# Block 0's queries come by GpSimd's queue: a chunk-selecting attention with a SwiGLU layer behind it

## The chip, the core and the metric

The kernel runs on one core of one Trainium2 chip. A core has five engines with an instruction queue each: TensorE (PE, matrix products), VectorE (DVE), ScalarE (ACT), GpSimd (POOL) and SyncE (SP, which only issues transfers here). Transfers between HBM and on-chip memory are started by SP, ACT or POOL and are carried by 16 DMA engines that all three share. The metric is the device time of one execution in microseconds (us); lower is better.

## What is computed

For 4 batches, 8 heads, 768 positions and 64 features per head, attention looks only at the six best chunks of 32 keys for each query, where a chunk is ranked by an upper bound from the least and the greatest of its keys, feature by feature. Its output, put together over the heads, goes through an RMS norm and a SwiGLU layer with 512 inputs and 1536 hidden features.

```
k_min, k_max = min and max of k over each chunk of 32 positions
ub    = sum_d max(q * k_min, q * k_max)            # one bound per query and chunk, causal
top   = the 6 chunks with the largest ub
attn  = softmax(q k^T / 8, causal, only keys of the chunks in top)
x     = (attn v), heads side by side               # 3072 tokens x 512
xn    = x / sqrt(mean(x^2) + 1e-6) * rms_g
out   = (silu(xn w_gate) * (xn w_val)) w_out       # 512 -> 1536 -> 512
```

## The kernel before, in words

The work is cut into 12 blocks of 256 tokens, `ORDER` in the code: block 0 is batch 0's first 256 positions, block 1 batch 1's, and so on. A block is named in operations by batch and third, so `(0, 0)` is block 0, `(1, 0)` block 1, `(2, 0)` block 2, `(0, 1)` block 4; a third figure is the group of four heads, of which there are two.

For each block the steps are: load k, q and v (`load_qk`, line 431; `load_v`, line 456). VectorE turns k and q so that features lie on partitions (`turn k`, `turn q`, line 636); ScalarE or GpSimd makes 16-bit copies of them (`half`, lines 643 and 644). VectorE takes each chunk's least and greatest key (`ext0`, `ext1`, line 651), GpSimd or VectorE writes them into small matrices (`dk`, line 657; `bd0`, `bd1`, line 676), and TensorE makes the bounds with them (`upper`, line 540), for which q's positive part is needed too (`relu`, lines 731 and 733). VectorE ranks (`ubn`, `bar`, `top`, `mk`, `mt`, lines 565 to 591). TensorE makes scores (line 760, with the mask at 771), ScalarE the exponentials (`exp`, line 810), GpSimd clears what lies above the diagonal (`tri`, line 780), TensorE multiplies with the values (`values`, line 836), VectorE normalises (`rden`, `norm`, lines 851 and 855). Then come the RMS norm (`square`, `rms`, `scale`, `turn`, `xsT`, lines 872 to 929) and the SwiGLU layer (`ffn`: `wg`, `wv` at line 960, `tanh`, `tg`, `vcopy`, `hh`, and `project` at line 1007).

For the first two blocks the norm and the layer run on half blocks, so that `xsT(0, (0,))` is block 0's first 128 tokens, ready for the first real matrices of the layer. Before that, and in gaps, TensorE is kept at work with multiplications that nobody reads (line 1074); they need the identity matrix `ident`, which GpSimd writes.

The order of the work is not decided on the chip. `Plan` collects all operations, each with a number, and the list `STEPS` says in which order they are written to their engines' queues: an entry is eight times the operation's number plus the engine, and a negative entry is a run of fill multiplications. Each engine works through its own queue in order and waits, by semaphores, for what an operation reads. `SLOTS` names the buffer that each tile takes. Both lists come from a search over the operations' assumed durations, made ahead of time.

Loads of k and q of the first three blocks are four transfers each, of 32 partitions, 128 KB (`PACKED`). All weights and values come by GpSimd's queue, converted to 16 bits on the way: `wg0` is the first third of the gate weights, `v000` and `v001` the two halves of block 0's values. `HELD = {2: ("wg", 1), 3: ("wo", 0)}` adds two waits: block 2's first load may not be issued before `wg1` has landed, and block 3's not before `wo0`. There are two buffers for raw k and three for raw q.

In the order before, SP issues two loads of block 0's k and two of its q, then block 1's; ACT issues the other two of each. GpSimd's queue begins with small clears, `ident`, `wv0`, `v000`, `wg1`, `v001`, `v100`, `wg0`.

Of the kernel before, what the change touches and what calls it, by code (L numbers as in the profile page):

```python
# [33 lines left out]
class Plan:  # L34
# [213 lines left out]
def kernel(  # L248
# [41 lines left out]
    def at(key):  # L290
        return store[plan.pool_of[key]][plan.slot[key]]
# [814 lines left out]
```

## Time and profile before

| | |
|---|---|
| Median of 3 runs | 294.74 us (293.15 to 296.25) |
| The profiled execution | 293.79 us |
| Its span in the profile | 292.1 us |
| TensorE busy | 279.0 us of the span |
| VectorE, ScalarE, GpSimd busy | 215.7, 207.1, 167.8 us |

The profile is one execution. Its span runs from the first instruction to the last; 1.69 us of the execution's time lie around it. Engine names are those above; PEld is TensorE's loading of weights, and a q behind an engine's name means its queue, where transfers are issued. A row of the timeline has start, length, engine, line, operation, output<-input, shapes and count, and in brackets the idle time before it with what ended that. Busy matrix products include the fill.

### The profile page before, as it was taken

What the parts mean: (1) busy time and instruction counts of PE and PEld (TensorE: products, weight loads), DVE (VectorE), ACT (ScalarE), POOL (GpSimd) and SP (SyncE); (2) the same over time, 40 slices, a digit from 0 to 9 for tenths busy, and PEclk for the clock granted to TensorE, in tenths of its full rate; (3) what the DMA queues carried; (4) which work ended last, traced back from release to release, by engine and by line L of the source; (5) the groups of instructions that cost most, each with busy time, mean ns of one, the idle gap of its engine ahead of it and who ended that gap; (6) DMA issues with size and microseconds to landing.
All of it is one profiled execution on the core that took longest, in us unless ns stands there. A gap on an engine that the chain in (4) does not pass through costs nothing.

```text
span 292.1 us, 11448 instructions
## 1 busy us (share of the span) xinstructions
PE 279.0 (96%) x4718; PEld 214.8 (74%) x4746; DVE 215.7 (74%) x626; ACT 207.1 (71%) x355; POOL 167.8 (57%) x268
## 2 busy tenths in 40 slices
PE   7979999999999899999999999999999999999994
PEld 7637887668877757888676786688678967688663
DVE  3778887889898799799989999987564715374240
ACT  2958887678888898877876595877679766564421
POOL 9649789879888785567683385427125116113410
PEclk9999999999999999999999999999999999999999
DMA  7999999988589584459599816912012300311022
GB/s 177 210 193 224 204 207 134 168 132 127 115 159 159 133 161 87 106 102 168 99 187 139 147 31 92 122 11 74 0 43 69 21 2 3 110 45 30 2 108 72
DMA packets 86388, 31.94 MB, mean 109 GB/s; under 512 B 74816, under 2 KB 81728, under 8 KB 86336
## 3 DMA queue, kind: packets, MB, share of 16 engines
q1 hardware_dynamic: 55776, 22.82, 33.9%
q0 software_dynamic: 29712, 7.87, 27.1%
q10 hardware_dynamic: 848, 0.53, 0.9%
q8 instruction: 37, 0.61, 0.9%
q14 instruction: 15, 0.12, 0.1%
HBM read 28.58 MB, written 6.29 MB: 119 GB/s over the span
## 4 chain that ended last, share of the span: by engine, by line
PE 84%; DMA 7%; DVE 5%; issue 2%; ACT 1%; DVEq 0%; SPq 0%
PE F L960 43%; PE F L1007 19%; PE S L760 7%; PE F L836 7%; DMA kraw<-in_k_dram 6%; PE S L771 3%; PE F L522 3%; DMA xsT<-xs 1%; PE F L540 1%; DVE kx L651 1%; DVE kT L636 1%; DVE xnat L855 1%; PE F L916 1%; DVE xs L890 1%; DVE tg L971 0%
## 5 line engine op out<-in xcount | busy, mean ns | idle before, releaser
L810 ACT ACTIVATE pt<-S 128x1024 bf16<-128x1024 f32 (+3 forms) x104 | 85.5, 858 | 29.7 <-PE S L771 26.4
L982 POOL TENSOR_TENSOR hh<-tg,vs 128x512 bf16<-128x512 bf16 x48 | 55.5, 1165 | 46.4 <-DVE tg L971 29.1
L960 PE MATMUL F<-xsT,wg 128*128 128x256 bf16 (+1 forms) x640 | 72.4, 262 | 0.2 <-DMA xsT<-xs 0.2
L960 PE MATMUL F<-xsT,wv 128*128 128x256 bf16 (+1 forms) x640 | 71.8, 262 | 0.6 <-issue 0.5
L1007 PE MATMUL F<-wo,hh 128*128 128x512 bf16 (+1 forms) x272 | 65.7, 370 | 2.3 <-issue 0.6
L971 DVE SCALAR_TENSOR_TENSOR tg<-th,F 128x512 bf16<-128x512 bf16 x72 | 48.3, 678 | 25.9 <-ACT th L967 19.6
L960 PEld LDWEIGHTS <-wg 128*128 128x128 bf16 x640 | 55.9, 98 | 9.2 <-issue 0.9
L960 PEld LDWEIGHTS <-wv 128*128 128x128 bf16 x640 | 56.2, 98 | 8.5 <-issue 1.0
L967 ACT ACTIVATE th<-F 128x512 bf16<-128x512 f32 x72 | 42.5, 599 | 13.9 <-PE F L960 12.6
L780 POOL TENSOR_SCALAR_AFFINE_SELECT pt<-pt 128x512 bf16<-128x512 bf16 x48 | 31.6, 665 | 27.9 <-ACT pt L810 27.7
L1007 PEld LDWEIGHTS <-hh 128*128 128x128 bf16 x300 | 27.5, 98 | 25.8 <-issue 1.0
L979 ACT ACTIVATE vs<-F 128x512 bf16<-128x512 f32 x48 | 28.5, 599 | 9.8 <-PE F L960 6.5
L760 PE MATMUL S<-qb,kb 32*128 32x256 bf16 (+1 forms) x800 | 32.8, 253 | 0.3
L651 DVE TENSOR_REDUCE kx<-kT 128x16 f32<-128x512 f32 x48 | 31.1, 669 | 0.2
L836 PE MATMUL F<-VX,pt 128*128 128x65 bf16 x672 | 27.5, 194 | 2.9 <-DMA VX<-in_v_dram 1.7
L836 PEld LDWEIGHTS <-pt 128*128 128x128 bf16 x672 | 25.4, 98 | 6.5 <-issue 3.3
L975 DVE TENSOR_TENSOR hh<-tg,F 128x512 bf16<-128x512 bf16 x24 | 16.1, 681 | 10.3 <-PE F L960 10.0
L760 PEld LDWEIGHTS <-kb 32*128 32x128 bf16 x800 | 13.6, 92 | 13.1 <-issue 11.6
L376 POOL DMA_DIRECT2D VX<-in_v_dram x24 | 22.7, 947 | 0.0
L771 PE MATMUL S<-mtd,chunkrow 32*128 32x128 bf16 (+2 forms) x384 | 20.3, 203 | 0.7 <-DVE xnat L855 0.7
L855 DVE TENSOR_TENSOR xnat<-F,rden 128x256 bf16<-128x256 f32 x48 | 19.5, 415 | 0.7
L771 PE MATMUL S<-mto,chunkrow 32*128 32x128 bf16 (+2 forms) x384 | 19.9, 203 | 0.0
(73 smaller groups left out, 337.3 us busy)
## 6 DMA issues: line engine op xcount, KB each, us to landing
out_dram<-osb SPq DMA_DIRECT2D x23, 256.0 KB, 3.0
kraw<-in_k_dram SPq DMA_DIRECT2D x72, 64.0 KB, 3.3
qraw<-in_q_dram SPq DMA_DIRECT2D x72, 64.0 KB, 3.1
VX<-in_v_dram POOLq DMA_DIRECT2D x24, 128.0 KB, 5.1
QX<-qT SPq DMA_DIRECT2D x32, 64.0 KB, 2.4
wv<-in_moe_w_val_dram POOLq DMA_DIRECT2D x3, 512.0 KB, 8.5
wg<-in_moe_w_gate_dram POOLq DMA_DIRECT2D x3, 512.0 KB, 13.5
wo<-in_moe_w_out_dram POOLq DMA_DIRECT2D x3, 512.0 KB, 10.2
```

The source lines that it names most:

```text
L651: plan.op(f"ext{n}{J}", "DVE", 0.585, 0.67, lambda n=n, op=op: VE.tensor_reduce(out=at(kx)[:, g, n], in_=at(kT).rearrange("p h (j c x) -> ...
L760: TE.matmul(s[a // 2][:, a % 2, c0:c0 + q1 - q0], kbt[r, t, ks], qbt[r, t, q0:q1], start=(t == 0), stop=(t == 1 and not mask), skip_group_ ...
L771: TE.matmul(o, chunkrow[r, BLK * kg + P * e:BLK * kg + P * (e + 1)], mv, start=False, stop=(d == 1), skip_group_check=True)
L780: GE.affine_select(out=d, in_=d, compare_op=ALU.is_ge, fill=0.0, base=0, pattern=[[0, 4], [1, P]], channel_multiplier=-1)
L810: lambda pt=pt, hs=hs, c0=c0, c1=c1, x=sc[hp]: SE.activation(out=at(pt)[:, hs, c0:c1], in_=at(x)[:, :, c0:c1], func=ACT.Exp, scale=SCALE), ...
L836: TE.matmul(o[:, a, :], p_[:, a, off:off + P], vt[:, e, 4 * g + a, :], start=(kb_ == 0 and a == 0), stop=(kb_ == nkb - 1 and a == 3), skip ...
L960: TE.matmul(at(p_)[:, n * W:(n + 1) * W], w[:, g, ht * P:(ht + 1) * P], at(xT)[:, g, x0:x0 + W], start=(g == 0), stop=(g == NP - 1), skip_ ...
L967: plan.op(f"tanh{U}.{hp}", "ACT", 0.48, 0.6, lambda th=th, gp=gp: SE.activation(out=at(th), in_=at(gp), func=ACT.Tanh, scale=0.5), pri - 0 ...
L971: VE.scalar_tensor_tensor(out=at(tg), in0=at(th), scalar=1.0, in1=at(gp), op0=ALU.add, op1=ALU.mult), pri - 30, reads=[th, gp], writes=[tg ...
L979: plan.op(f"vcopy{U}.{hp}", "ACT", 0.48, 0.6, lambda vs=vs, vp=vp: SE.activation(out=at(vs), in_=at(vp), func=ACT.Copy), pri + 0.1, reads= ...
L982: plan.op(f"hh{U}.{hp}", "POOL", 1.11, 1.16, lambda tg=tg, vs=vs, hh=hh: GE.tensor_tensor(out=at(hh), in0=at(tg), in1=at(vs), op=ALU.mult) ...
L1007: TE.matmul(at(op)[:, cs], at(key)[:, o:o + P], wo[:, ht, cs], start=(ht == 0), stop=(ht == NHT - 1), skip_group_check=True)
```

## The change

Block 0's four q loads, until now issued by SP and ACT (two each), are issued by GpSimd, with the same shape. A second way of cutting a load, `WHOLE`, is written but used for nothing (the set is empty). The rest of the edit is the two lists, searched anew.

```diff
+    WHOLE = set()
+    BYPOOL = {(0, 'q')}
...
         key = (nm + "raw", b, m)
-        first = True
-        for a in (0, 2, 1, 3):
-            rows = slice(32 * a, 32 * (a + 1))
-            if i in PACKED:
-                sv = src[b].rearrange("(g a) (m r j) d -> a m r g (j d)", a=4, m=NBLK, r=32)[a, m]
-                todo = [(sv, lambda rows=rows: at(key)[rows].rearrange("r g j h d -> r g (j h d)"), 4, 0.12, (0, 1))]
...
-                dma(f"load {nm}{b}{m}{a}{k_}", ("SP", "ACT") if i == 0 else ("SP",), sv, dst, packets, cost,
...
+        todo = []
+        if (i, nm) in WHOLE:
...
+        else:
+            for a in (0, 2, 1, 3):
+                rows = slice(32 * a, 32 * (a + 1))
+                if i in PACKED:
+                    sv = src[b].rearrange("(g a) (m r j) d -> a m r g (j d)", a=4, m=NBLK, r=32)[a, m]
+                    todo.append((f"{a}0", sv, lambda rows=rows: at(key)[rows].rearrange("r g j h d -> r g (j h d)"),
+                                 4, 0.12, (0, 1)))
+                    continue
...
+        first = True
+        engs = ("POOL",) if (i, nm) in BYPOOL else ("SP", "ACT") if i == 0 else ("SP",)
+        for x, sv, dst, packets, cost, gs in todo:
+            dma(f"load {nm}{b}{m}{x}", engs, sv, dst, packets, cost,
+                loads_due(i, nm == "q"), writes=[key + (g,) for g in gs],
+                takes=[(key, nm + "raw")] if first else (), reads=() if first else [key],
+                behind=[HELD[i]] if i in HELD and first else ())
+            first = False
...
     STEPS = (
-        123, 228, 233, 155, 3, 99, 249, 244, 27, 257, 276, 83, 34, 203, 139, 281, 67, 268, 107, 315,
...
     SLOTS = (
-        0, 0, 1, 1, 0, 1, 0, 0, 1, 0, 0, 0, 0, 1, 1, 0, 1, 0, 0, 1, 2, 3, 0, 0, 0, 1, 1, 0, 1, 0, 0,
...
```

Written out by engine, the start of the new order is:

- GpSimd: the four q loads of block 0, `ident`, three clears and `ones0`, `v001`, `v000`, `eps`, `wg0`, two `ones` and a clear, `dk`, `bd0`, `bd1` of `(0, 0, 0)`, `wv0`, `bd1(0, 0, 1)`, `wg1`, `v100`, `wv1`, `v101`, then the two `tri` of block 0 with which the first `values` are made.
- SP: two loads of block 0's k, then block 1's: three of k, two of q, one of k, two of q; then block 2's, all k before q, with one small load of block 4's k among them.
- ACT: the other two loads of block 0's k, then its copies.
- VectorE: `own` (it needs `ident`), `turn k` of both groups, `ext0` and `ext1` of group 0 with `own8` between, `turn q` of group 0, `ext1` of group 1, `turn q` of group 1, `pat`, `ext0` and `dk` of group 1, `ubn` to `mk` of group 0, one `bd0`, then `turn q(1, 0, 0)`, ahead of block 0's second ranking; `turn k(1, 0, 0)` and `turn q(1, 0, 1)` stand among that ranking. `xsT(0, (0,))` is the 48th entry of this queue, as before.
- TensorE: 46 small fill products ahead of the first real work, where there were 92; the sum of larger ones is 34 in both. The rest is the same work with neighbours exchanged; `upper(2, 0, 0)` stands behind `wv(0, (0,)).8` and `wg(1, (0, 1)).4`, which followed it before.

More of the change, by code (lines that the diff above doesn't have):

```diff
@@ L433, in load_qk @@
         key = (nm + "raw", b, m)
-        first = True
-        for a in (0, 2, 1, 3):
-            rows = slice(32 * a, 32 * (a + 1))
-            if i in PACKED:
-                sv = src[b].rearrange("(g a) (m r j) d -> a m r g (j d)", a=4, m=NBLK, r=32)[a, m]
-                todo = [(sv, lambda rows=rows: at(key)[rows].rearrange("r g j h d -> r g (j h d)"), 4, 0.12, (0, 1))]
-            else:
-                todo = []
+        todo = []
+        if (i, nm) in WHOLE:
+            for g in range(NG):
+                sv = src[b].rearrange("(g a) (m r j) d -> g m a r (j d)", g=NG, m=NBLK, r=32)[g, m]
+                todo.append((f"g{g}", sv, lambda g=g: at(key)[:, g].rearrange("p j h d -> p (j h d)"), 8, 0.09, (g,)))
+        else:
[6 more added lines that the diff above has]
+                    continue
@@ L442, in load_qk @@
                 for g in range(NG):
                     sv = src[b, 4 * g + a, BLK * m:BLK * (m + 1), :].rearrange("(j r) d -> r j d", r=32)
-                    todo.append((sv, lambda rows=rows, g=g: at(key)[rows, g].rearrange(
+                    todo.append((f"{a}{g}", sv, lambda rows=rows, g=g: at(key)[rows, g].rearrange(
                         "r j h d -> r j (h d)"), 16, 0.019, (g,)))
-            for k_, (sv, dst, packets, cost, gs) in enumerate(todo):
-                dma(f"load {nm}{b}{m}{a}{k_}", ("SP", "ACT") if i == 0 else ("SP",), sv, dst, packets, cost,
-                    loads_due(i, nm == "q"), writes=[key + (g,) for g in gs],
-                    takes=[(key, nm + "raw")] if first else (), reads=() if first else [key],
-                    behind=[HELD[i]] if i in HELD and first else ())
-                first = False
+        first = True
```

276 rows, old and new, of tables (SLOTS, STEPS) are left out of this document.

## Prediction

> **What bounds the kernel now.** I read the page first, for what carries the chain that ended last.
>
> ```profile
> span 292.1 us, 11448 instructions
> PE 279.0 (96%) x4718; PEld 214.8 (74%) x4746; DVE 215.7 (74%) x626; ACT 207.1 (71%) x355; POOL 167.8 (57%) x268
> PE 84%; DMA 7%; DVE 5%; issue 2%; ACT 1%; DVEq 0%; SPq 0%
> ```
>
> TensorE carries 84% of the chain; the 7% of transfers must stand somewhere in particular. The chain in order of time says where, and the table of stretches says how dense each stage is (columns: stretch, length, busy time of PE, PEld, DVE, ACT, POOL with instruction counts, granted clock, share of the DMA engines, GB/s).
>
> ```profile
> 0.80 3.05 DMA kraw<-in_k_dram
> 3.87 5.78 DMA kraw<-in_k_dram
> 9.67 7.49 DMA kraw<-in_k_dram
> 17.24 1.31 DVE kT L636 x2
> 25.43 1.79 PE F L960 x32
> ```
>
> ```profile
> 0.00:5.09 5.09, 3.09 (x30) 3.10 (x31) 0.29 (x2) 1.28 (x1) 4.41 (x20) 1.00 0.58 160
> 5.09:13.40 8.31, 8.18 (x158) 6.29 (x160) 7.90 (x28) 6.52 (x12) 5.74 (x12) 1.00 1.33 212
> 13.40:17.24 3.84, 2.11 (x47) 1.28 (x47) 0.72 (x3) 1.88 (x6) 1.35 (x3) 1.00 1.42 201
> 17.24:25.27 8.03, 7.64 (x157) 4.23 (x155) 7.95 (x28) 6.11 (x13) 6.47 (x16) 1.00 1.54 212
> 25.27:60.00 34.73, 33.44 (x654) 28.46 (x653) 28.04 (x80) 27.26 (x52) 30.61 (x49) 1.00 1.10 178
> 60.00:287.57 227.57, 224.20 (x3688) 171.38 (x3713) 170.81 (x490) 163.26 (x273) 119.27 (x173) 1.00 0.49 89
> ```
>
> From 60 us on TensorE is busy 224.20 of 227.57 us: only 3.37 us can be had there. Until the layer's first matrices, in the chain at 25.43, most of its busy time is fill. In that head VectorE is the full engine (7.90 of 8.31, 7.95 of 8.03), except from 13.40 to 17.24, where it worked 0.72 of 3.84 us. Its timeline shows the hole:
>
> ```profile
> 5.09 1.30 DVE L636 STREAM_TRANSPOSE kT<-kraw 128x512 f32<-128x512 f32 x2 [2.83 <-DMA kraw<-in_k_dram]
> 8.07 0.71 DVE L636 STREAM_TRANSPOSE qT<-qraw 128x512 f32<-128x512 f32 x1 [0.16 <-DMA qraw<-in_q_dram]
> 12.17 0.30 DVE L565 STREAM_TRANSPOSE ubn<-F 128x32 f32<-128x32 f32 x2
> 13.16 0.24 DVE L591 STREAM_TRANSPOSE mtd<-mk 128x64 bf16<-128x64 bf16 x1
> 16.27 0.71 DVE L636 STREAM_TRANSPOSE qT<-qraw 128x512 f32<-128x512 f32 x1 [2.87 <-DMA qraw<-in_q_dram]
> 17.24 1.31 DVE L636 STREAM_TRANSPOSE kT<-kraw 128x512 f32<-128x512 f32 x2 [0.25 <-DMA kraw<-in_k_dram]
> 19.62 0.24 DVE L851 RECIPROCAL rden<-F 128x4 f32<-128x4 f32 x2
> 24.19 0.69 DVE L929 TENSOR_TENSOR xsT<-F,rmsg 128x512 bf16<-128x512 bf16 x1
> ```
>
> Block 0 is ranked by 13.40, and block 1's q and k come at 16.27 and 17.16: 2.87 + 0.25 = 3.12 us lost. The chain tells why they come late: they leave at 3.87 to 9.67, each step beginning where an older load landed. The first issue at 3.87 is the ninth load on SP and ACT together, and SP's own waits confirm that it waits for loads (us, times, longest):
>
> ```profile
> SPq L376 <- DMA kraw<-in_k_dram: 5.4, 5, 1.7
> ```
>
> **GpSimd's start.** Four loads are put ahead of all else on GpSimd's queue, and `ident` behind them. GpSimd's rows, and what TensorE does with `ident`:
>
> ```profile
> 0.80 0.31 POOL L420 MEMSET BO<- 128x256 f32 x1 [0.29 <-POOLq L1090]
> 1.37 0.20 POOL masks.py:197 MEMSET ident<- 128x128 bf16 x1
> 2.79 0.97 POOL L376 DMA_DIRECT2D wv<-in_moe_w_val_dram  x1
> 5.23 0.77 POOL L376 DMA_DIRECT2D wg<-in_moe_w_gate_dram  x1
> 5.97 1.79 POOL L376 DMA_DIRECT2D VX<-in_v_dram  x2
> 11.53 0.64 POOL L780 TENSOR_SCALAR_AFFINE_SELECT pt<-pt 128x512 bf16<-128x512 bf16 x1 [0.21 <-ACT pt L810]
> 2.00 7.19 PE L1074 MATMUL F<-ident 128*128 128x128 bf16 x92 [2.00 <-POOL ident masks.py:199]
> ```
>
> GpSimd is held 0.77 to 0.97 us by one issue; at 0.9 (1.79 for two) four take it from 0.80 to 4.4, and `ident`, 0.63 us long (1.37 to 2.00), is there at 5.0 (4.5 to 5.3). VectorE's `own` stands first in its queue and needs `ident`: 0.29 us (the busy time of the first stretch), so its first `turn k` begins near 5.3 where it was 5.09. I charge 0.2 us. TensorE's 46 fill products, at 7.19/92 = 0.08 us each, end at 8.6; half of the warm-up is cut, but the first real product waits for q's copy anyway:
>
> ```profile
> 6.43 2.09 ACT L643 ACTIVATE kb<-kT 128x512 bf16<-128x512 f32 x2 [2.46 <-DVE kT L636]
> 8.82 2.10 ACT L643 ACTIVATE qb<-qT 128x512 bf16<-128x512 f32 x2 [0.30 <-DVE qT L636]
> ```
>
> One such copy is 1.05 us, so with q turned at 8.8 the first scores stand near 9.85, past the fill's end: nothing. If the cover goes, it is because the fill ends later, and each us is paid once.
>
> **When q lands.** Loads of block 0's kind on GpSimd are not in the trace. The rows for bounds (transfers, count, size written, us from issue to landing):
>
> ```profile
> qraw<-in_q_dram SPq DMA_DIRECT2D x1, 128.0 KB, 5.5
> wv<-in_moe_w_val_dram POOLq DMA_DIRECT2D x1, 512.0 KB, 8.3
> VX<-in_v_dram POOLq DMA_DIRECT2D x1, 128.0 KB, 12.0
> kraw<-in_k_dram SPq DMA_DIRECT2D x1, 128.0 KB, 7.5
> wg<-in_moe_w_gate_dram POOLq DMA_DIRECT2D x1, 512.0 KB, 13.5
> ```
>
> Nearest is `wv`, first on GpSimd's queue as these will be, and 512 KB as the four are together: 0.80 + 8.3 = 9.1. Early bound: the fourth, issued at 0.80 + 3 x 0.9 = 3.5, lands as soon after as the first k load did, 3.05 us by the chain: 6.6; with the 5.5 us of SP's q load it would be 9.0. Late bound: `VX`, which had `wv` ahead of it, 3.5 + 12.0 = 15.5. `wv` is converted from twice the bytes, so I take 8.0. VectorE comes to `turn q` at 8.07 - 0.16 + 0.2 = 8.1: no cost, and 1.0 us if it lands at 9.1.
>
> **When block 1 lands.** Eight loads were out before SP first waited; with q gone, four of block 1's join block 0's four k loads at once, and the other four follow as those land, by about 5.3 us instead of 9.67. The bytes ahead of the last of them are 16 loads of 128 KB, 2.1 MB. At the stretches' rates 0.81 MB are through by 5.09 (160 GB/s) and the rest, 1.29 MB at 212 GB/s, 6.1 us later: 11.2. `v001` and `v000` share that time; if they cost what a 7.5 us load shows against a 5.5 us one, 2 us, it is 13.2. I take 12.3. VectorE now meets `turn q(1, 0, 0)` ahead of block 0's second ranking, which is some 1.2 us (12.17 to 13.40 in the old order), so at 12.2 + 0.2. New wait: 0 to 1.0, taken at 0.3.
>
> So of the 3.12 us, 0.2 and 0.3 are given back there. Behind it the first `values` need `v000` and the triangles. These waited before:
>
> ```profile
> 16.41 0.42 PE L836 MATMUL F<-VX,pt 128*128 128x65 bf16 x8 [1.73 <-DMA VX<-in_v_dram]
> ```
>
> The first `tri` now stands behind eight more issues: 5.0 + 8 x 0.9 and some 2 us of small work, 14.2, and the second ends at 15.5 (0.64 each). `v000`, the second issue after 0.9 us of clears, leaves near 6.8; 8.3 to 12.0 us to landing is 15.1 to 18.8, taken near the early end since no weights are ahead of it. So `values` start near 15.5, and VectorE asks for the result at 19.62 - 2.6 = 17.0. Cost 0.3, as the late end would be 2 us. VectorE's 47 entries ahead of the first `xsT` are nearly the same work; I put nothing for them. The layer's first matrix thus moves from 25.43 by 3.12 - 0.2 - 0.3 - 0.3 = 2.3 us.
>
> **What is late next.** Block 2's loads wait for `wg1`, now ninth on GpSimd's queue instead of third, and all of SP's queue waits with them. Before, it landed at 5.23 + 13.5 = 18.7.
>
> ```profile
> 33.32 1.29 DVE L636 STREAM_TRANSPOSE kT<-kraw 128x512 f32<-128x512 f32 x2
> 40.39 0.44 PE L540 MATMUL F<-qT,BO 64*64 64x32 f32 x16
> ```
>
> Block 2's k was turned at 33.32 without any waiting for data, and its bounds were made at 40.39. Two matrices of the layer (1.79 us for two) now stand ahead of these bounds, so TensorE comes to them at 40.39 + 1.8 - 2.3 = 39.9; the 7.1 us from `turn k` to bounds mean that k may be turned at 32.8. `wg1` lands at 19 to 22: q by 8.0, two value loads at 1 to 2.5 us, three weights at about 2.9 (0.52 MB of each over 178 GB/s). Block 1's eight loads took 13.3 us (3.87 to 17.16), so the five that hold block 2's k take 8 to 10 and end at 27 to 32: enough for the bounds, but VectorE's order wants k sooner than it did. Give-back 0 to 2, taken at 0.5.
>
> **The rest.** From 60 us TensorE's order is the old one with neighbours exchanged; 0, within 1 either way. Sum against the profiled execution: 293.79 - 2.3 + 0.5 = 292.0. The shown runs' median lies 0.95 above that execution, which by the same 1.8 us gives 292.9. I name 292.4.
>
> **The rivals.** The first: only bytes count. The row: the DMA engines' share is 1.33 to 1.54 from 5.09 on, so they hardly rest. Then block 1 is sooner only by what steps behind it, `wv0`'s 512 KB: 0.52 MB / 212 GB/s = 2.5 us, so 14.7 for 17.16. The engines' busy share is above 1 as packets overlap. VectorE stands from 12.4 on, and the 1.2 us of ranking follows: gain 2.5 - 1.2 = 1.3, less 0.2: 292.7. Against it: the 5.4 us of SP's waits, which this removes. The Trainium skill says this in "DMA: Bandwidth & Descriptors", section "Issuing engines are not separate DMA queues": transfers started by different engines run interleaved on the same 16 DMA engines, and starting from more engines saves only issuing time. By that rule alone the 5.4 us would be worth nothing; the trace agrees with the sharing, while the waits it shows are for landings, not for issuing.
>
> The second: everything comes through. No new wait, and half of the 34.73 - 33.44 = 1.29 us that TensorE rests between 25.27 and 60 goes too: 3.12 + 0.6 = 3.7, so 290.1. For it: VectorE had no DMA waits but these. Against it: `ident` and `v000`.
>
> The third, slower: q is late on GpSimd's queue, at the `VX` price. Then `turn q(0, 0, 0)` holds VectorE from 8.1 to 15.5, and everything of blocks 0 and 1 is queued behind it: 7.4 - 3.12 + 0.2 = 4.5 us, 298.3. It decides from a landing at 8.1 + 3.12 - 0.2 = 11.0 on. For it: value and weight loads on that queue all took 8.3 us and more. Against it: these four are first, with nothing ahead. A `wg1` at 25 or later would do the same in smaller measure, through block 2.
>
> **How the numbers follow.** Forecast 0.38 (own range 291 to 294), bytes alone 0.15, all comes through 0.29, q late 0.18. A measurement of this kernel tells about 1%, 2.9 us. Faster by more is the second rival, 0.29; the forecast and the first lie within 1%, 0.53; slower by more is the third, 0.18. The range reaches from 289.3, the second rival's price with a little more idle time gone, to 296.3, past the point where the third begins to cost, leaving its upper part out.
>
> **What would show it.** Right: VectorE's q turn near 8.0 with little idle time; no idle time over 1 us before the second block's turns, at 12 to 13; the first product of line 960 near 23 in the chain; SP's waits for k loads nearly gone, and its wait for `wg1` in their place. Wrong: a DMA wait of VectorE at the first q turn; TensorE idle in 35 to 50 us while block 2 arrives; or an end that moves differently from the start of line 960, which would put the difference into the new order.

## The result: slower by two thirds of a per cent

| | before | after |
|---|---|---|
| Median | 294.75 us (20 runs, 292.99 to 299.14) | 296.64 us (20 runs, 294.66 to 298.96) |
| Ratio | | 1.0067, 95% interval 1.0040 to 1.0093 |
| Profiled execution, its span | 293.79 us, 292.1 us | 294.77 us, 292.4 us |

The forecast was 292.4 us, 289.3 to 296.3; the time lies above the range. Of the 1.89 us between the medians, 0.61 stand outside the span: the time around it was 1.71 us in the mean of the runs before and 2.32 after. The rest must be found inside.

Ratios here leave out runs more than 1.5% above the fastest of their kernel; where a kernel's times spread wide, that leaves out many (5 of 12 in e5, 7 of 12 in e7 and in e8), and its median, which is of all runs, says more.

The page after, its span, its busy time and the chain by engine:

```profile
span 292.4 us, 11365 instructions
...
PE 276.7 (95%) x4671; PEld 212.8 (73%) x4700; DVE 216.4 (74%) x626; ACT 211.0 (72%) x364; POOL 166.4 (57%) x263
...
PE 81%; DMA 6%; DVE 6%; ACT 3%; issue 2%; SPq 1%; POOL 0%; DVEq 0%; ACTq 0%; POOLq 0%
```

TensorE carries three points less of the chain than before, VectorE and ScalarE more. To see where, the same stretches of both kernels (stretch, length, busy time of PE, PEld, DVE, ACT, POOL, TensorE's granted clock as a share of full speed, share of the DMA engines, GB/s); length less PE is TensorE's idle time. Before:

```profile
0.00:12.00 12.00, 9.87 (x172) 8.87 (x176) 6.92 (x21) 6.55 (x8) 9.59 (x30) 1.00 0.98 194
12.00:30.00 18.00, 15.19 (x324) 9.66 (x325) 13.82 (x54) 13.11 (x31) 12.93 (x26) 1.00 1.39 206
30.00:100.00 70.00, 67.94 (x1153) 53.70 (x1158) 60.18 (x181) 57.43 (x107) 59.62 (x92) 1.00 0.93 154
100.00:165.00 65.00, 63.75 (x1264) 48.37 (x1269) 59.67 (x194) 49.07 (x82) 40.65 (x63) 1.00 0.78 132
```

And after:

```profile
0.00:12.00 12.00, 6.31 (x88) 5.88 (x89) 5.90 (x14) 5.65 (x7) 8.27 (x26) 1.00 1.15 204
12.00:30.00 18.00, 17.57 (x384) 11.36 (x382) 16.24 (x58) 14.23 (x33) 15.57 (x29) 1.00 1.35 201
30.00:100.00 70.00, 69.08 (x1151) 54.38 (x1147) 63.78 (x190) 58.59 (x109) 58.51 (x92) 1.00 0.93 153
100.00:165.00 65.00, 60.96 (x1234) 46.35 (x1241) 55.68 (x175) 50.96 (x85) 37.09 (x57) 1.00 0.62 124
```

The first row has 3.56 us less, all but the 46 fill products left out (46 x 0.08 = 3.7), which are no work. From 12 to 30 us TensorE's idle time falls from 2.81 to 0.43 us, from 30 to 100 from 2.06 to 0.92: 3.5 us less in all. Not all of that is work: with every fill product left out (lines 1074 and 1083), TensorE has 79.0 us of products behind it at 100 us, where it had 76.9, so the kernel is 2.1 us ahead there. From 100 to 165 us its idle time rises from 1.25 to 4.04. VectorE's timeline after shows what it met, at the start and late (idle time before a row and its cause in brackets):

```profile
4.83 1.30 DVE L645 STREAM_TRANSPOSE kT<-kraw 128x512 f32<-128x512 f32 x2 [0.17 <-DMA kraw<-in_k_dram]
...
8.90 0.71 DVE L645 STREAM_TRANSPOSE qT<-qraw 128x512 f32<-128x512 f32 x1 [1.53 <-DMA qraw<-in_q_dram]
...
12.51 0.22 DVE L596 TENSOR_TENSOR mk<-ubn,m 128x64 bf16<-128x64 f32 x1
...
12.75 0.70 DVE L645 STREAM_TRANSPOSE qT<-qraw 128x512 f32<-128x512 f32 x1
...
14.16 0.71 DVE L645 STREAM_TRANSPOSE kT<-kraw 128x512 f32<-128x512 f32 x1
...
14.91 1.91 DVE L742 TENSOR_SCALAR qraw<-qT 128x128 f32<-128x128 f32 x1
15.30 1.52 DVE L596 TENSOR_TENSOR mk<-ubn,m 128x64 bf16<-128x64 f32 x1
...
24.25 0.68 DVE L938 TENSOR_TENSOR xsT<-F,rmsg 128x512 bf16<-128x512 bf16 x1
...
31.15 1.31 DVE L645 STREAM_TRANSPOSE kT<-kraw 128x512 f32<-128x512 f32 x2
...
128.02 0.71 DVE L645 STREAM_TRANSPOSE qT<-qraw 128x512 f32<-128x512 f32 x1 [1.21 <-DMA qraw<-in_q_dram]
...
143.55 0.71 DVE L645 STREAM_TRANSPOSE kT<-kraw 128x512 f32<-128x512 f32 x1 [1.89 <-DMA kraw<-in_k_dram]
```

Lines of the new kernel are 9 further down than those of the old (636 is 645). Two waits for data stand at 128 and 143 us, where the old kernel had none, and TensorE's timeline shows what hung on them: VectorE's `hh` was queued behind each turn. (Its first row here is the first product with block 0's data.)

```profile
10.78 0.29 PE L769 MATMUL S<-qb,kb 32*128 32x128 bf16 x8 [1.31 <-ACT qb L652]
...
16.21 0.30 PE L845 MATMUL F<-VX,pt 128*128 128x65 bf16 x4 [0.20 <-POOL pt L789]
...
24.98 1.05 PE L969 MATMUL F<-xsT,wv 128*128 128x128 bf16 x16
...
129.96 0.92 PE L845 MATMUL F<-VX,pt 128*128 128x65 bf16 x24 [1.43 <-DVE hh L984]
...
146.51 1.03 PE L969 MATMUL F<-xsT,wv 128*128 128x256 bf16 x8 [1.23 <-DVE hh L984]
```

These are loads of block 9, `(3, 1)`: `q3110` and `k3131` (batch, third, partitions' quarter, group), each the last of its half tile in SP's queue. And at 14.91 VectorE's `relu` took 1.91 us and `mk` 1.52, where a `mk` of the same shape took 0.22 at 12.51; the last of GpSimd's rows explains the end of both at 16.8 (1.27 us for two `tri`, which follow an issue without a pause):

```profile
1.40 2.35 POOL L378 DMA_DIRECT2D qraw<-in_q_dram  x4 [0.90 <-POOLq L1099]
3.74 0.22 POOL masks.py:197 MEMSET ident<- 128x128 bf16 x1
...
14.57 0.91 POOL L378 DMA_DIRECT2D VX<-in_v_dram  x1
15.46 1.27 POOL L789 TENSOR_SCALAR_AFFINE_SELECT pt<-pt 128x512 bf16<-128x512 bf16 x2
```

The old kernel's first product of the layer, in its TensorE timeline:

```profile
25.27 1.05 PE L960 MATMUL F<-xsT,wg 128*128 128x128 bf16 x16
```

So the layer starts only 0.29 us sooner (24.98), and the kernel ends later: the forecast's own sign that the difference lies in the new order. Another of its signs of being wrong, a wait of VectorE at the first q turn, is there too (1.53 us).

### The profile page after: what moved, and what is told of

Same layout as the page of the kernel before. It is cut to its first block, busy times and chain, and to the rows that moved or that the text cites. A ratio compares the mean times of both kernels' runs of the same rounds, so it can differ in the third digit from the quotient of the medians.

```text
span 292.4 us, 11365 instructions
## 1 busy us (share of the span) xinstructions
PE 276.7 (95%) x4671; PEld 212.8 (73%) x4700; DVE 216.4 (74%) x626; ACT 211.0 (72%) x364; POOL 166.4 (57%) x263
## 4 chain that ended last, share of the span: by engine, by line
PE 81%; DMA 6%; DVE 6%; ACT 3%; issue 2%; SPq 1%; POOL 0%; DVEq 0%; ACTq 0%; POOLq 0%
PE F L969 40%; PE F L1016 18%; PE S L769 7%; PE F L845 7%; DMA qraw<-in_q_dram 3%; PE F L531 3%; PE S L780 3%; PE F L549 2%; PE F L1083 2%; DMA out_dram<-osb 2%; DMA kraw<-in_k_dram 1%; DVE kx L660 1%; ACT pt L819 1%; DVE qraw L742 1%; DVE qT L645 1%
## 5 line engine op out<-in xcount | busy, mean ns | idle before, releaser
L991 POOL TENSOR_TENSOR hh<-tg,vs 128x512 bf16<-128x512 bf16 x48 | 56.1, 1173 | 39.4 <-ACT vs L988 21.2
L1016 PE MATMUL F<-wo,hh 128*128 128x512 bf16 (+1 forms) x271 | 64.6, 370 | 3.1 <-POOL hh L991 0.6
L976 ACT ACTIVATE th<-F 128x512 bf16<-128x512 f32 x72 | 41.7, 601 | 16.9 <-PE F L969 16.4
L645 DVE STREAM_TRANSPOSE qT<-qraw 128x512 f32<-128x512 f32 x24 | 16.7, 698 | 4.5 <-DMA qraw<-in_q_dram 2.9
```

The costliest lines, as they stand in the source:

```text
L976: plan.op(f"tanh{U}.{hp}", "ACT", 0.48, 0.6, lambda th=th, gp=gp: SE.activation(out=at(th), in_=at(gp), func=ACT.Tanh, scale=0.5), pri - 0 ...
L991: plan.op(f"hh{U}.{hp}", "POOL", 1.11, 1.16, lambda tg=tg, vs=vs, hh=hh: GE.tensor_tensor(out=at(hh), in0=at(tg), in1=at(vs), op=ALU.mult) ...
L1016: TE.matmul(at(op)[:, cs], at(key)[:, o:o + P], wo[:, ht, cs], start=(ht == 0), stop=(ht == NHT - 1), skip_group_check=True)
```

## The experiments

All changes are shown by the names of operations in an engine's queue. "Head" is the order up to block 3's last product with the values (`values(3, 0, 1)1`, at some 74 us), "rest" what follows. Differences between two experiments are differences of their ratios.

**Which part costs.** Theory A: the new order of the rest loses what the head gains. Theory B: the move itself costs. Four kernels take the change apart.

```diff
 e1, old order:  POOL: + q0000 q0010 q0020 q0030, ahead of all
                 SP:   - q0010 q0020      ACT: - q0000 q0030
                 PE:   46 small fill products for 92
 e2, new order:  POOL: - the four q loads   SP, ACT: + two each;  PE: 92 for 46
 e3:  new head, old rest
 e4:  old head, new rest
```

> The old order with block 0's four q loads moved to the front of GpSimd's queue, and the first fill cut to 46 products as in the changed kernel, since ident comes later; nothing else is reordered. Theory A (the new order of the rest loses what the head gains): block 1 lands near 10.5 us instead of 17.2, VectorE's 3.1 us of waiting goes and 0.8 us come at the first q turn (8.9 for 8.07); with the old order's turns behind the ranking the first product of line 960 stands 1.5 to 2.5 us sooner than 25.3, and the time is 0.992 to 0.997 of before. Theory B (the move itself costs: late ident, late q, a later start of TensorE): 1.003 to 1.008, and line 960 starts no sooner.

> The changed kernel with block 0's q loads back on SP and ACT, two each behind the k loads, and the first fill back at 92 products, since ident comes early again; all else in the new order. Theory A: block 1's data come near 17 us again, and the new order wants them ahead of block 0's second ranking, so the head loses 3 to 4 us against the changed kernel: 1.015 to 1.02 of before. Theory B: the move was the loss, so this is at or below before: 0.995 to 1.003.

> The changed kernel up to block 3's last product with values (near 85 us), the old order from there on. Theory A: the changed kernel stood 0.7 us ahead at 85 us and lost 1.4 and 1.2 us at two waits of TensorE near 130 and 147 us; without them 0.994 to 0.999 of before, and no gap of TensorE above 0.5 us between 100 and 160 us except the old one near 99. Theory B: the loss is in the head, so 1.004 to 1.008 as the changed kernel.

> The old kernel up to block 3's last product with values, the new order from there on; q by SP and ACT as before. Theory A: the gaps near 130 and 147 us appear here too, shifted by under 1 us, and the time is 1.005 to 1.01 of before. Theory B: 0.998 to 1.003, as the head is the old one.

| | median us | before beside it | ratio, 95% interval |
|---|---|---|---|
| e1, move alone | 293.25 | 294.93 | 0.9950, 0.9912 to 0.9988 |
| e2, new order without the move | 298.31 | 294.93 | 1.0109, 1.0055 to 1.0163 |
| e3, new head, old rest | 295.31 | 294.93 | 1.0008, 0.9969 to 1.0047 |
| e4, old head, new rest | 296.12 | 294.93 | 1.0038, 1.0000 to 1.0076 |

The move alone gains half a per cent. With either head the new rest adds 0.4 to 0.6% (1.0038 against 1, 1.0067 against 1.0008; each difference is about as large as its uncertainty). But the new head takes back what the move gains: e3 stands 0.0058 above e1 (uncertainty 0.005) and misses the 0.994 to 0.999 that theory A gave it. Theory B falls, and A is half of the account, without a mechanism yet. The windows of e1 show most of the changed kernel's gain up to 100 us (78.5 us of products without the fill), and none of its loss behind (idle 0.34, 0.74, 0.72 us):

```profile
12.00:30.00 18.00, 17.66 (x405) 11.81 (x405) 15.65 (x63) 14.99 (x34) 13.76 (x28) 1.00 1.41 197
30.00:100.00 70.00, 69.26 (x1152) 54.53 (x1150) 61.38 (x186) 58.39 (x109) 59.91 (x93) 1.00 0.94 156
100.00:165.00 65.00, 64.28 (x1286) 47.72 (x1285) 59.80 (x196) 49.77 (x82) 41.39 (x63) 1.00 0.78 136
```

**Is it the clock?** TensorE's granted clock, averaged over a run, was 0.9919 over the runs after and 0.9966 to 0.9977 over the four sets of runs before that stand beside the experiments. In e3's profile the loss is seen directly, in stretches of 3.41 us at half clock behind two idle gaps of TensorE, whose rows are first:

```profile
10.77 0.40 PE L769 MATMUL S<-qb,kb 32*128 32x128 bf16 x8 [2.26 <-ACT qb L652]
...
133.58 1.88 PE L969 MATMUL F<-xsT,wg 128*128 128x256 bf16 x8 [1.72 <-DMA xsT<-xs]
```

```profile
10.75:14.16 3.41, 3.39 (x45) 1.67 (x44) 2.61 (x12) 2.94 (x6) 2.23 (x4) 0.50 1.61 191
...
133.63:137.04 3.41, 3.41 (x17) 2.43 (x18) 2.04 (x18) 0.60 (x1) 3.41 (x6) 0.50 0.52 142
```

This third theory, C, was tested by filling the first gap, in the changed kernel and in e1:

```diff
 e5, changed kernel, PE:  46 small fill products ahead of the first real one -> 62
 e6, e1, PE:              46 -> 60
```

> The changed kernel with 62 small fill products ahead of the first real work instead of 46, so that TensorE has work in the 1.31 us between 9.47 and 10.78 in which it waited for q's copy. Theory C (gaps of TensorE bring windows of half clock, and the difference in mean clock, 0.9919 against 0.9975, is most of the loss): one gap less, so fewer windows; mean clock 0.995 or more, time 295.5 to 296.0, ratio near 1.002. Theory A (the order of the later work loses, by loads that come late to VectorE at 128 and 143 us): the gap at 10 us costs nothing, ratio stays at 1.006 to 1.008, mean clock near 0.992.

> The move alone with the old order (e1), with 60 small fill products instead of 46. In e1 the fill ended at about 10.0 and the first real product stood at 10.83, with a second gap of 0.77 at 12.04. Theory C: mean clock goes from 0.9951 to 0.997 or more, and the time from 293.25 to about 292.5, ratio 0.992. Rival: the start is set by q's landing at 9.9 and the second gap stays, so ratio 0.995 as in e1; if the fill is too long it delays the first bounds by up to 0.4 us and the ratio is 0.996.

e5: the mean clock rose to 0.9956, the time did not fall: 296.91 us, ratio 1.0057 (1.0020 to 1.0093). e6: the clock rose from 0.9941 to 0.9972 over all runs, 293.63 us, ratio 0.9975 (0.9945 to 1.0006), no better than e1. The gain that theory C asked for in e5, 0.004, is no larger than the uncertainty, so this alone would not refute it; but e13 and e14 below have mean clocks of 0.990 and 0.993 and are faster than the kernel before them at 0.997. The clock is not the whole cause.

It is not out of the account either. Among runs of one kernel those at a lower mean clock were longer, by 1.6 to 2.1 us for each 0.01 (lines fitted over all kernels, each about its own mean; the smaller figure is for the runs in the ratios). By this estimate the 0.005 between the two kernels goes with about 1 us of the 1.89; no run here tells which of the two brings the other. The profiles show where much of it is lost. Fourteen of the kernels here have q on GpSimd's queue. In nine of their profiles TensorE stood idle for 1.37 us or more ahead of its first real products and ran at half clock within some 2 us of that gap; in the five others (the changed kernel, e1, e5, e6, e7) the longest such gap was 1.31 us and the clock stayed full. A length alone is no rule: the kernel before had a gap of 1.73 us at 16.41 and kept its clock. What it can do to the head is seen in e7 and e14 below, whose orders up to 100 us are the same. VectorE made `xsT(0, (0,))` at 23.36 us in e7's profile, at full clock, and 2.4 us later in e14's, where the clock stood at 0.51 from 10.82 to 17.65 us and q had been turned 0.4 us later:

```profile
23.36 0.69 DVE L938 TENSOR_TENSOR xsT<-F,rmsg 128x512 bf16<-128x512 bf16 x1
```

```profile
25.80 0.69 DVE L938 TENSOR_TENSOR xsT<-F,rmsg 128x512 bf16<-128x512 bf16 x1
```

**The stretch at 15 us.** In e7 the two operations are taken out of GpSimd's way:

```diff
 e7, changed kernel
-DVE: ... top(0,0,1) relu(1,0,0) mk(0,0,1) turn q(1,0,1) ext0(1,0,0) ...
+DVE: ... top(0,0,1) turn q(1,0,1) ext0(1,0,0) mk(0,0,1) ...
+ACT: ... swap(0,0,0) relu(1,0,0) ...
```

> The changed kernel with the operations taken apart that ran into GpSimd at 14.9 us: relu(1, 0, 0) goes to ScalarE, and VectorE makes turn q(1, 0, 1) and ext0(1, 0, 0), which did not stretch beside GpSimd, before mk(0, 0, 1). Theory D (VectorE's relu and mk took 1.91 and 1.52 us because GpSimd was issuing and running tri): VectorE has turned q(1, 0, 1) by 15.7 instead of 17.4, the first product of the layer starts near 23.8 to 24.2 instead of 25.0, and the end comes 0 to 1 us sooner, as TensorE loses later what it gains here (theory A): ratio 1.003 to 1.007. Rival (the 1.9 us was a wait for something else, such as data): the same operation waits as long on ScalarE, or mk is stretched wherever it stands, and the first product of the layer stays at 25.0.

VectorE's timeline of e7:

```profile
14.73 0.69 DVE L645 STREAM_TRANSPOSE qT<-qraw 128x512 f32<-128x512 f32 x1
15.35 0.64 DVE L660 TENSOR_REDUCE kx<-kT 128x16 f32<-128x512 f32 x1
15.91 0.73 DVE L596 TENSOR_TENSOR mk<-ubn,m 128x64 bf16<-128x64 f32 x1
```

The turn and `ext0` run at their usual length beside GpSimd; `mk`, put later, still met the second `tri` and took 0.73; `relu`, on ScalarE, took 0.43 at 14.91, so it had not been waiting for data. q is turned by 15.4 instead of 17.4, and the first product of the layer starts at 24.10 (24.98 in the changed kernel), as expected:

```profile
24.10 1.05 PE L969 MATMUL F<-xsT,wv 128*128 128x128 bf16 x16
```

The Trainium skill, "SBUF — State Buffer", section "Who interferes with whom", says which kinds are held up by GpSimd on a shared port (a `tensor_scalar` in certain modes, a `tensor_tensor` with both inputs in SBUF while GpSimd reads there) and that a `tensor_reduce` is not; `mk`, a `tensor_tensor`, and `ext0`, a `tensor_reduce`, agree. Yet the median was 296.22 us, no lower than the changed kernel's against its own runs before (+1.89 us in both; 294.33 us before, beside e5 to e8). The ratio of 0.9999 (0.9954 to 1.0044) says little, as the times spread from 291.48 to 300.30. The profiled execution was the quickest, so the gain can reach the end; over all its runs the mean clock was 0.9895, lower than the changed kernel's, and one late load still waited (1.34 us at 140). Which of the two kept the gain from the median is open.

**The late loads.** e8, e10 and e11 ask after the two waits at 128 and 143 us.

```diff
 e8, changed kernel, SP:   q3110 up ahead of k1220;  q3121 k3101 k3131 up ahead of q2221
 e10, changed kernel, SP:  loads of k and q in the old order among themselves
 e11, e1, SP:              loads of k and q in the new order among themselves
```

In e10 and e11 the exchange covers the loads behind operation `values(0, 1, 1)1`; the expectations put that at 75 us, but the first load that differs is issued at 102.

> The changed kernel with four loads moved up in SP's queue by 3 to 8 places: load q3110 ahead of load k1220, and load q3121, k3101, k3131 ahead of load q2221. VectorE waited for these, 1.21 us at 128.0 and 1.89 us at 143.6, and hh and TensorE behind it (1.43 and 1.23 us). Theory A (the new order's later part loses by its late loads): both waits shrink below 0.5 us, TensorE's gaps at 130 and 147 go, and the time falls by 1 to 2 us, ratio 1.000 to 1.003. Theory C: fewer gaps also mean a higher mean clock, 0.994 or more. Rival (the end of VectorE's queue is late anyway; something else takes the place): waits go, the gaps stay or come elsewhere, ratio 1.006.

> The changed kernel, in which from 75 us on SP's loads of k and q stand in the old order among themselves; every other queue is the changed kernel's. Theory A, by its late loads: VectorE's waits for data at 128 and 143 us (1.21 and 1.89 us) go, TensorE's idle time between 100 and 165 us falls from 4.0 to about 1.5 us, and the time by 1 to 2 us, ratio 1.000 to 1.004. Rival (the old order of loads does not fit the new order of VectorE, or the loss lies elsewhere in the order): waits for data at other turns, ratio 1.006 or more.

> The move alone (e1), in which from 75 us on SP's loads of k and q stand in the new order among themselves: the suspected cause put into the kernel that lacks it. Theory A, by its late loads: VectorE waits 1 to 4 us in all for k and q between 120 and 150 us, where e1 waited for none, TensorE's idle time between 100 and 165 us rises from 0.7 to 2 us or more, and the ratio goes from 0.995 to 1.000 or more. Rival: VectorE waits, but TensorE has other work, ratio 0.995 to 0.997.

e8 missed: its ratio, 1.0026 (0.9980 to 1.0071), lies in the range of theory A, but its median, 297.06 us, is 2.73 us above its runs before, where the changed kernel's is 1.89 above. VectorE waited for neither load, but the moved loads had pushed back the transfers of `qm` (queries laid out anew for the positive part) in SP's queue, and ScalarE waited for one, as its timeline shows:

```profile
141.45 0.63 ACT L740 ACTIVATE qraw<-QX 128x512 f32<-128x512 f32 x1 [3.25 <-DMA QX<-qT]
```

e10 and e11 came out 3 to 4 us above the kernel before: 298.74 us, ratio 1.0126 (1.0092 to 1.0160), and 298.04 us, ratio 1.0117 (1.0081 to 1.0153). In e10 TensorE's idle time between 100 and 165 us did go, to 0.31 us, but VectorE then waited 4.57 us, first row; in e11 it waited 3.18 us, second row, and TensorE 2.68 us behind it:

```profile
167.73 0.71 DVE L645 STREAM_TRANSPOSE kT<-kraw 128x512 f32<-128x512 f32 x1 [4.57 <-DMA QX<-qT]
```

```profile
120.95 0.71 DVE L645 STREAM_TRANSPOSE qT<-qraw 128x512 f32<-128x512 f32 x1 [3.18 <-DMA qraw<-in_q_dram]
```

So the order of SP's queue and those of the engines that it feeds are a pair, with little slack between them. But neither shows the price of the two waits in the changed kernel. For that the loads had to come sooner without anything urgent going back; here only loads of later blocks do, and `k3120` by one place, while `qm` moves up too:

```diff
 e13, changed kernel, SP
-... q3120 q3130 k1220 k3120 k1210 q3110 k3130 across50 across51 q3101 q3111 q2200 qm0 k3121 qm2
-    k3110 q2221 k3200 q3121 q2210 qm1 qm3 q2220 store3.1 q2201 k3101 k3131 ...
+... q3120 q3130 q3110 k1220 k1210 k3120 k3130 across50 across51 q3101 q3111 qm0 k3121 qm2
+    k3110 q3121 qm1 qm3 store3.1 k3101 k3131 q2200 q2221 k3200 q2210 q2220 q2201 ...
 e14:  e13 and e7 together
 e15:  e4 (old head, new rest) with e13's edit
```

> The changed kernel with the late loads made sooner without passing any transfer of qm: six loads of the blocks after them (q2200, q2221, k3200, q2210, q2220, q2201) go behind k3131, k3120 behind k1210, q3110 ahead of k1220. In e8 the four moved loads had pushed the two transfers of qm back, and ScalarE waited 3.25 us for them at 141 us. Theory A, by its late loads: no wait of VectorE or ScalarE for a transfer over 0.5 us between 120 and 150 us, TensorE's idle time between 100 and 165 us below 2 us (4.0 in the changed kernel), time 1 to 2 us below the changed kernel's, ratio 1.000 to 1.003. Rival (SP's queue is full, so that whatever goes first, something comes late): the six loads are late in their turn, VectorE waits for them at 155 to 165 us, ratio 1.005 or more.

> e13 and e7 together: the changed kernel without VectorE's stretch at 15 us and without the late loads. Theories A and D together: the head's gain of 1 us is kept, ratio 0.994 to 0.998. Rival (the new order loses elsewhere): no lower than e13, 1.000 or more.

> e4 (old head, new order from the fourth block's values on) with e13's edit, so that the new rest is mended and stands against e4's 1.0038 and the kernel before. Theory A, by its late loads: ratio 0.998 to 1.001. Rival: 1.003 or more.

| | median us | before beside it | ratio, 95% interval |
|---|---|---|---|
| e13 | 294.20 | 295.16 | 0.9980, 0.9952 to 1.0007 |
| e14 | 292.80 | 295.16 | 0.9939, 0.9909 to 0.9969 |
| e15 | 292.98 | 295.16 | 0.9951, 0.9924 to 0.9979 |

The two turns of e13, in VectorE's timeline, and its TensorE between 100 and 165 us (idle 2.21 us, 4.04 before the edit):

```profile
128.31 0.71 DVE L645 STREAM_TRANSPOSE qT<-qraw 128x512 f32<-128x512 f32 x1
...
142.34 0.70 DVE L645 STREAM_TRANSPOSE kT<-kraw 128x512 f32<-128x512 f32 x1
```

```profile
100.00:165.00 65.00, 62.79 (x1251) 47.95 (x1257) 57.37 (x179) 52.81 (x89) 37.17 (x57) 1.00 0.61 124
```

Both waits are gone. What is left is a wait of 0.65 us at 138 in e13, and one near 162 us (1.67 us in e13, 1.89 in e15; 1.54 us stood there in the changed kernel too).

The edit takes 0.0087 off the ratio in the changed kernel (1.0067 to 0.9980) and the same 0.0087 behind the old head (1.0038 to 0.9951), each with an uncertainty of 0.004 to 0.005: some 2.6 us. The spread shrinks as well (292.0 to 295.1 us in e13). That is more than the 1.8 us of idle time by which the two profiles differ, and more than expected; 0.33 us of it lies outside the span (1.99 us for 2.32). It is not the clock's doing, as e13's mean clock is no higher than the changed kernel's. And it is the price against the same order with its loads in time, not against the old rest: mended, the new rest is better than the old one, for e15 has the old head, without the move, and stands at 0.9951. The profiled execution of the changed kernel, 294.77 us, was among its quickest; in the profile of e5, whose order is the same, VectorE waited almost twice as long at the same turn of k:

```profile
145.86 0.71 DVE L645 STREAM_TRANSPOSE kT<-kraw 128x512 f32<-128x512 f32 x1 [3.47 <-DMA kraw<-in_k_dram]
```

With the two waits gone, the mended head seems to pay: e14 is 0.0041 below e13 (uncertainty 0.004). It has the lowest ratio of the study, 0.6% below the kernel before and 1.3% below the changed one. Most of the 0.6% is the mended rest: e15, without the move, is only 0.0012 behind, less than the uncertainty.

**What is left in the head.** e9 shares q out, e12 puts e7's edit into e3, e16 joins the two.

```diff
 e9, e1:   POOL: - q0020 q0030;  ACT: + q0020 q0030, behind its k loads
 e12, e3:  e7's edit
 e16, e12: e9's edit
```

> The old order with block 0's q shared out: two loads on GpSimd's queue, first, and two on ScalarE's behind its k loads, where e1 has all four on GpSimd's. In e1 the four were issued by 3.73 us and landed at 9.87, and the fill could not start before 4.94 because ident stood behind them. Theory E (in e1 the start of TensorE and the landing of q cost the head; the gain lies in block 1's loads, which no longer wait for a landing): ident is about 1.1 us earlier, q is issued by 2.7 and lands 0.5 to 1 us earlier, block 1 about 1 us later than in e1, since two of its loads must wait for a landing again; time 0 to 0.7 us below e1's, ratio 0.992 to 0.995. Rival (the bytes ahead of it decide): q lands at 9.5 to 10 all the same, ratio 0.995 to 0.997.

> The new head with the old order behind it (e3), with e7's edit: relu(1, 0, 0) on ScalarE, turn q(1, 0, 1) and ext0(1, 0, 0) ahead of mk(0, 0, 1). Theory D: the layer starts about 0.9 us sooner than in e3, as it did in e7 against the changed kernel, and the old rest, which has its loads in time, keeps it: 0.5 to 1.2 us below e3's 295.31, ratio 0.997 to 0.999. Rival (the new head loses by something else than this stretch, for instance by what block 2 finds): ratio 1.000 to 1.003, with the first product of the layer sooner all the same.

> e12 (new head without the stretch, old rest) with q shared out as in e9, two loads on GpSimd's queue and two on ScalarE's. Theory E: the fill starts at 3.3 instead of 4.4 us, q is turned 0.3 to 0.6 us sooner than in e12 (8.95), while block 1's last loads wait for landings again; as the new head makes turn q(1, 0, 0) early, it may wait for data there. Ratio 0.993 to 0.997. Rival: q's landing does not move, or block 1 loses what q gains; ratio 0.996 to 0.999.

e9: 293.80 us, ratio 0.9968 (0.9938 to 0.9998). q's first turn came at 8.53 for 9.99 in e1, the fill at 3.90, but the gain stayed out; block 1's loads had to wait for landings again, and TensorE then stood idle for 1.37 and 1.19 us. e12: 293.77 us, ratio 0.9963 (0.9933 to 0.9993), 0.0045 below e3 (uncertainty 0.005). With e14 that is the second time that the gain of theory D shows where the rest has its loads in time, each time no larger than its uncertainty. e16: 294.00 us, ratio 0.9986 (0.9964 to 1.0008), no better than e12. It missed its purpose: q's first turn came at 9.94, not sooner than e12's 8.95, and TensorE waited 3.41 us for its copy. What an earlier q would be worth under the new head is open.

## Why the prediction failed, step by step

The three experiments that take the change apart give the sum of the forecast in its own terms. The move gains 0.50% (e1), 1.5 us where 1.8 were forecast. The new head, put at nothing beside the old one, costs 0.58% (e3 against e1), and the new rest, put at nothing, 0.59% (the changed kernel against e3; 0.38% by e4): some 1.7 us each, with uncertainties nearly as large. Those two terms are where the forecast failed. Term by term:

- **GpSimd's start**, charged 0.2 us: wrong in sign and small. The issues began at 1.40, not 0.80, but four took 2.35 us, not 3.6: a load that is not converted took 0.53 to 0.75 us, the converted ones 0.77 to 0.97. `ident` was written from 3.74 on, and the first turn stood at 4.83, where it was 5.09.
- **q at 8.0, no cost**: the mechanism was right, the size was not. The chain has the landing at 3.21 + 5.56 = 8.77, and VectorE and then TensorE waited, 1.53 us and 1.31 us; the turn stood 0.83 us later than before. This is inside the bounds, and below the 11.0 at which the slower rival began. Two of the forecast's own rows gave 9.0 and 9.1; it took less, by an argument on conversion that no row showed.

```profile
3.21 5.56 DMA qraw<-in_q_dram
...
8.90 0.72 DVE qT L645
```

- **Half of the warm-up cut, "nothing"**: this failed too, in part. The fill ended at 9.47 and the first real product came at 10.78, not 9.85. That gap is the one behind which other executions fell to half clock; what it cost the changed kernel is not measured, about 1 us by the estimate above.

- **Block 1 at 12.3, the hole of 3.12 us goes**: right, and better than priced. Its last load had landed by 11 us (issued by 5.2, and 5.7 us to landing), and VectorE turned its q at 12.75 and its k at 14.16 without any wait for data. SP's waits for k in the first 25 us, which are block 1's, went from the first row (before) to the last, with the wait for `wg1` in their place. Over the first 60 us, the window of the forecast's 5.4, they are 4.4: later blocks' loads still wait for landings.

```profile
SPq L376 <- DMA kraw<-in_k_dram: 3.7, 4, 1.4
```

```profile
SPq L378 <- DMA wg<-in_moe_w_gate_dram: 15.2, 1, 15.2
...
SPq L378 <- DMA kraw<-in_k_dram: 0.3, 1, 0.3
```

- **"VectorE's 47 entries ahead of the first `xsT` are nearly the same work; I put nothing for them"**: this failed. They are the same work at other times, and two of them now lay beside GpSimd's issue and triangles: 1.91 us for `relu` and `mk`, of which e7 got 0.9 back at the layer's start. That start moved by 0.29 us, not 2.3; q's later turn (0.83) and the stretch account for most of the difference.
- **`values` near 15.5, 0.3**: 16.21, with 0.20 us for `tri`. Near enough.
- **Block 2, give-back 0.5**: SP's wait of 15.2 us ended at 20.83, when its first load left (row below), within the 19 to 22 given for `wg1`; VectorE turned its k at 31.15 without a wait. No give-back.

```profile
20.83 2.97 SPq L378 DMA_DIRECT2D kraw<-in_k_dram  x5
```

- **"From 60 us on TensorE's order is the old one with neighbours exchanged; 0, within 1 either way"**: this failed, and here the cause is shown. SP's loads were exchanged too, and two of them landed after VectorE had come to them, 1.21 and 1.89 us late, with TensorE behind it. With its loads in time the same rest is 0.87% faster, some 2.6 us, under either head (e13, e15). The prediction looked at TensorE's order alone, and the list of who is queued behind whom stopped at block 2.
- The rival "only bytes count" is refuted by the landing: block 1 had landed by 11 us, where that rival had it at 14.7. e1's time, 0.5% below the kernel before, does not tell it from the forecast, as it priced a gain of 1.1 us. "Everything comes through", at 290.1, lies below every median here. After both repairs e14's 292.80 us is close to the 292.4 forecast, but that is in good part luck: much of its gain is the mended rest, which the forecast did not have. "Late on GpSimd's queue" had the direction and the right kind of event, a load that VectorE meets too late, with all else queued behind it, but not the load: q landed at 8.77.

Open: the 0.61 us around the span. Kernels with the old rest had 1.70 to 1.83 us there, those with the new one 1.9 to 2.4; no run looked into it. Open too is how much of the loss is the clock's. And the start of the layer proved a poor measure of the head: in e1's profile it stands at 25.29, no sooner than before, where 1.5 to 2.5 us had been expected, and e1 is 0.5% faster.

## What to carry to other kernels

When an order is searched anew, price every queue that changed, the transfer queue above all, and not only the engine that is the bound: two loads that came one to two microseconds after their reader cost more here than the early stage gained. Test a move alone under the old order before believing a new order that comes with it, and mend each half alone: e15 showed that the better part of the best kernel was the new rest, not the move. One profile is one execution: the same head reached the layer 2.4 us apart in two of them, with the granted clock beside it, so read the clock of a stretch before comparing its times.

## What the hardware showed that was not expected

- VectorE's `relu`, 0.28 and 0.33 us in the kernel before, took 1.91 us beside GpSimd and ended at 16.82, as GpSimd's third instruction in a row did at 16.73 (an issue and two triangles). A second `relu` of the changed kernel, at 41.08, took 0.91 and ended at 41.99, where GpSimd's `hh` ended at 41.86. Turns and reductions of VectorE ran beside the same instructions at 0.64 to 0.71 us.
- TensorE's clock halved for 3.41 us behind idle gaps of 2.26 and 1.72 us in e3, and in e12 behind one of 1.47, but not behind one of 1.73 in the kernel before. The Trainium skill, "TensorE: Matmul & The Clock Gate", Part 1, gives an idle window of about 3.4 us as the condition and says that the window runs freely; the length agrees, the gaps here were shorter. Raising the mean clock from 0.992 to 0.996 (e5) changed the time by less than could be measured, while among runs of one kernel 0.01 of it went with 1.6 to 2.1 us.
